# A fused window attention and two dense layers on one core: the reciprocal sums move to the PSUM banks of P^T, and the first loads are issued from two queues

## Chip, cores and metric

The kernel runs on one core of a Trainium2 chip. The metric is the device time of one execution in microseconds (us). TensorE is called PE here, VectorE DVE, ScalarE ACT, GpSimd POOL, and SyncE SP, as in the profile; PEld is PE's weight load, which has rows of its own.

## What is computed

Windowed causal attention (4 batches, 8 heads, 576 positions, head size 64, a window of 128 keys and a linear position bias), then two dense layers of 512 to 2048 to 512 on the 2304 rows that result. The first layer's activation is a quotient of polynomials, the second's a squared ReLU.

```python
scores = scale * q @ k.T                      # per head
scores = where(0 <= rel < 128, scores - slope * abs(rel), -1e9)
attn = exp(scores - max); attn /= attn.sum() + 1e-9
x = (attn @ v)                                # 2304 x 512
h = x @ w_in;   g = (a0 + a1 h + a2 h^2 + a3 h^3) / (1 + |b0||h| + |b1| h^2 + 1e-6);  y = g @ w_out
h = y @ w2_in;  g = max(h, 0)^2;  out = g @ w2_out
```

The weights come as 64-bit floats, so the kernel rebuilds each 32-bit value from two words.

## The kernel before

**Attention** works on 16 pairs of heads. For a pair, q and k are loaded as 128x4x128 blocks. PE transposes four q blocks into one PSUM bank (`tr_main`, line 337; called trq below), ACT or DVE copies the bank to `qkT` (`tr_copy`), the same follows for k (trk), and for the last 64 queries and keys together (`tr_rem`, trr). Three groups of score matmuls (`s_pe`) write four banks, five query tiles in all. DVE adds the bias and takes the row bound (`ttr`, line 383, tile `e`). ACT takes the exponential and its row sum (`exp`, into `sums`). PE transposes the probabilities (`pt_pe`, P^T, called ptp), and ACT or DVE copies them (`pt_copy`, called ptc, tile `ptsb`). PE multiplies by v (`pv_pe`) into bank `o`. The last 64 queries go into a bank `or`, which also holds the transposed reciprocal sums. `rcp` adds 1e-9 to the nine sums of a pair and takes the reciprocal, both on DVE. `r_tr` (plan name rtp) transposes them on PE into `or`. `r_copy` copies them out as `rt`, and `x_copy` copies `o` (plan name xo) and the last queries (xr) into `xT`. The result is stored unnormalised beside the reciprocals.

**PSUM** has eight banks here, handed out by `bank` (line 243): tag `s` has four, `pt` two (P^T), `o` one, `tr` one. trq, trk, trr and `or` take turns in the one bank `tr`.

**Weights** are rebuilt in 64 chunks beside all this: four steps on DVE, ACT or POOL (lines 206 to 218, tile `wb`) and a split into a rounded high part and a rest (lines 222 to 229). Eleven bits of precision in each part make three matmuls out of one.

**The dense layers** run in blocks of 512 rows (one of 256) and 16 steps per block: `gemm_in` (line 685) fills one of the four `s` banks (tile `h`) with 12 matmuls, some nine elementwise instructions on ACT, POOL and DVE follow, which end with `gl` on DVE, and `gemm_out` accumulates `y` in the banks of `pt`, `o` and `tr`. Step f of `gemm_in` needs the bank of step f-4, and so its `gl`. The first four steps need the score banks of the last pair.

**What sets the order** is the class `Plan` (lines 16 to 97). Every operation has its predecessors, a cost for each engine that may run it, and a priority. `run` takes again and again the operation that could start first by these costs; as `WEIGHT` is 0, the priority, with a number from the table `BIAS` added for each kind of operation, only decides between equal starts. The order found is written out, and each engine then works through its own list in order.

Of the kernel before, what the change touches and what calls it, by code (L numbers as in the profile page):

```python
# [8 lines left out]
F32 = mybir.dt.float32  # L9
# [3 lines left out]
ALU = mybir.AluOpType  # L13


class Plan:
# [30 lines left out]
    def run(self):  # L47
# [9 lines left out]
        while ready:  # L57
            best = None
            for name in ready:
                _, after, prio, engs, _, port = self.ops[name]  # L60
# [21 lines left out]
            if eng == "Pool" or (eng == "DVE" and self.ops[name][5]):  # L82
                free["port"] = max(free.get("port", 0.0), end - self.PORT[eng])
            if eng == "SP":
                free["DMA"] = max(free.get("DMA", 0.0), end + self.QUEUE) + self.ops[name][4]
                end = free["DMA"] + self.DONE
# [12 lines left out]

BIAS = {'W0': -416.9, 'W1': -833.9, 'W2': 174.9, 'W3': -153.9, 'attn_end': 896.0, 'bias': -332.0, 'exp': 84.0, 'g1': 159.6, 'g2': 163.5, 'gh': 2.9, 'gl': -268.1, 'ldk': 57.5, 'ldk0': -338.4, 'ldq': 99.3, 'ldq0': 331.9, 'ldr': 377.8, 'ldv': 105.8, 'ptc': -247.7, 'ptp': 268.5, 'pv': 64.8, 'r_abs': 33.0, 'r_g1': 63.2, 'r_g2': -144.0, 'r_g3': -694.3, 'r_p1': 486.9, 'r_p2': 266.4, 'r_r1': 109.8, 'r_r2': 206.0, 'r_t1': -202.8, 'r_t2': -379.6, 'r_u': -91.6, 'rcp': -171.9, 'rout': 202.1, 'rtc': -511.3, 'rtp': -541.3, 's': -127.0, 's_g': -91.3, 's_relu': -222.2, 'scl': -214.7, 'scp': 712.6, 'trk': 99.1, 'trk0': 101.2, 'trk0c': -324.6, 'trkc': 290.0, 'trq': -28.9, 'trq0': -378.1, 'trq0c': -90.4, 'trqc': 356.2, 'trr': 192.3, 'trrc': -666.1, 'ttr': -675.7, 'w0': 396.4, 'w1': 108.0, 'w2': 400.3, 'w3': -491.9, 'w4': -326.2, 'w5': -103.3, 'warm': 442.5, 'wl': -405.2, 'x': 124.7, 'xh': -413.4, 'xl': -200.5, 'xld': -1.2, 'xn': -207.3, 'xo': 145.8, 'xr': 36.3, 'yc': -225.0, 'yo': -531.9}  # L100
WEIGHT = 0.0000
# [7 lines left out]
def tile_window_attention_moe_moe(  # L109
# [20 lines left out]
    nc = tc.nc  # L130
# [169 lines left out]

    def load_qk(p, nme, src, t0, t1):
        b, hp = pairs[p]
        h0 = 2 * hp
        if t0 == 0:
            st[p][nme] = araw.tile([P, NQ - 1, 2, D], F32, tag=f"{nme}r", name=f"{nme}r{p}")
        t = st[p][nme]
        for j in range(2):
            nc.sync.dma_start(
                t[:, t0:t1, j, :], src[b, h0 + j, t0 * P : t1 * P, :].rearrange("(t p) d -> p t d", p=P)
            )  # L310

# [190 lines left out]
    for p in range(NP):  # L502
# [54 lines left out]
        for i in range(NQ):  # L557
# [3 lines left out]
            for j in range(2) if i < NQ - 1 else (1,):  # L561
# [6 lines left out]
                    ("exp", u, j), lambda u=u, j=j: exp(u, j), ACT=(0.49, 0.44, 0.39)[part],  # L568
                    after=[("ttr", u, j), ("rcp", p - 3)], prio=u,
# [21 lines left out]
        plan.add(("rtp", p), lambda p=p: r_tr(p), PE=0.08, after=[("rcp", p), ("trkc", p + 2), ("trrc", p + 1), ("xr", p - 1)], prio=u0 + 4.2)  # L591
        plan.add(
# [352 lines left out]
```

## Time and profile before

| | us |
|---|---|
| three runs | 943.40, 943.42, 945.23 |
| median | 943.42 |
| profiled execution | 942.65 |
| its span in the trace | 940.9 |
| PE busy | 923.6 (98%) |
| DVE busy | 625.9 (67%) |
| ACT busy | 494.9 (53%) |
| POOL busy | 324.0 (34%) |

The page also cuts the span into 40 slices with the busy share of each engine, lists the costliest groups of instructions, and follows the chain of work that ended last. Of that chain 87% lies on PE: 42% are the matmuls of line 778 (`y`) and 40% those of line 694 (`h`). A matmul's busy time overlaps with the next one's, so a PE that is busy all the time isn't at its peak by that alone; what counts is from one start to the next. The first 146 us are attention, the rest are the dense layers.

### The profile page before, as it was taken

To read this page: it belongs to the slowest core of one execution; us is meant where nothing else is said; L and a number is where in the kernel's file an instruction comes from. 1 tells how busy PE (TensorE), PEld (TensorE's weight loads), DVE (VectorE), ACT (ScalarE), POOL (GpSimd) and SP (SyncE) were. 2 spreads that over 40 slices of the span, in tenths; PEclk is the share of its full clock that TensorE was granted. 3 is DMA by queue.
4 is the path that set the end of the run, shared out by engine and by line. 5 is a ranking of instruction groups with operands and counts; after the bars stand their busy time and mean duration, and the time that the engine had idled before them with its cause. 6 is when DMAs were issued, how large, how long until landed. Compare 5 with 4: busy or idle time off the path is not lost.

```text
span 940.9 us, 14096 instructions
## 1 busy us (share of the span) xinstructions
PE 923.6 (98%) x4908; PEld 759.5 (81%) x4908; DVE 625.9 (67%) x1285; ACT 494.9 (53%) x1072; POOL 324.0 (34%) x343
## 2 busy tenths in 40 slices
PE   7999999999999999999999999999999999999998
PEld 5666667888998888888888888888888888888897
DVE  3999998999888886887799987862233223222232
ACT  4988887767767555655666654432222222222222
POOL 5354236867455446444666731030010001000000
PEclk9999999999999999999999999999999999999999
DMA  8999963322402100400142254302000200100010
GB/s 183 236 227 242 241 190 120 115 91 67 132 27 78 35 1 1 125 10 1 37 143 90 68 179 160 133 23 89 1 1 16 74 0 1 68 1 1 1 45 22
DMA packets 102311, 77.01 MB, mean 82 GB/s; under 512 B 64465, under 2 KB 89441, under 8 KB 102241
## 3 DMA queue, kind: packets, MB, share of 16 engines
q1 hardware_dynamic: 102240, 76.12, 28.7%
q8 instruction: 38, 0.62, 0.3%
q14 instruction: 33, 0.26, 0.1%
HBM read 61.87 MB, written 14.23 MB: 81 GB/s over the span
## 4 chain that ended last, share of the span: by engine, by line
PE 87%; DVE 8%; ACT 3%; DMA 1%; issue 1%; SPq 0%; POOL 0%; POOLq 0%; DVEq 0%; ACTq 0%
PE y L778 42%; PE h L694 40%; DVE e L391 3%; ACT e L407 2%; PE tr L340 1%; PE pt L442 1%; DVE wb L218 1%; PE warm L613 1%; DVE qkT L291 1%; DVE wb L216 1%; DMA win1r<-in_moe_w_in_dram 1%; DMA wout1r<-in_moe_w_out_dram 1%; PE o L468 0%; DVE ptsb L291 0%; DVE win1r L214 0%
## 5 line engine op out<-in xcount | busy, mean ns | idle before, releaser
L222 ACT ACTIVATE gh<-h 128x512 fp32r<-128x512 f32 (+1 forms) x160 | 88.7, 555 | 182.4 <-PE y L778 153.4
L229 DVE TENSOR_TENSOR gl<-h,gh 128x512 fp32r<-128x512 f32 (+1 forms) x160 | 101.7, 636 | 122.3 <-ACT gh L222 121.7
L755 DVE SCALAR_TENSOR_TENSOR h<-h,ah 128x512 f32<-128x512 f32 (+1 forms) x80 | 51.6, 645 | 115.0 <-ACT ah L751 114.8
L694 PE MATMUL h<-xh,win1hi 128*128 128x512 f32 (+1 forms) x320 | 118.1, 369 | 1.0 <-DVE gl L229 1.0
L694 PE MATMUL h<-xl,win1hi 128*128 128x512 f32 (+1 forms) x320 | 117.8, 368 | 0.0
L778 PE MATMUL y<-gh,wout1hi 128*128 128x512 f32 (+1 forms) x320 | 117.8, 368 | 0.0
L778 PE MATMUL y<-gl,wout1hi 128*128 128x512 f32 (+1 forms) x320 | 117.7, 368 | 0.0
L694 PE MATMUL h<-xh,win1lo 128*128 128x512 f32 (+1 forms) x320 | 117.7, 368 | 0.0
L778 PE MATMUL y<-gh,wout1lo 128*128 128x512 f32 (+1 forms) x320 | 117.7, 368 | 0.0
L694 PE MATMUL h<-xh,win2lo 128*128 128x512 f32 (+1 forms) x320 | 117.7, 368 | 0.0
L694 PE MATMUL h<-xl,win2hi 128*128 128x512 f32 (+1 forms) x320 | 117.7, 368 | 0.0
L694 PE MATMUL h<-xh,win2hi 128*128 128x512 f32 (+1 forms) x320 | 117.6, 368 | 0.0
L778 PE MATMUL y<-wout2hi,gh 128*128 128x512 f32 x288 | 112.2, 390 | 0.0
L778 PE MATMUL y<-wout2hi,gl 128*128 128x512 f32 x288 | 112.2, 390 | 0.0
L778 PE MATMUL y<-wout2lo,gh 128*128 128x512 f32 x288 | 112.1, 389 | 0.0
L751 ACT ACTIVATE ah<-h 128x512 f32<-128x512 f32 (+1 forms) x80 | 44.4, 554 | 120.9 <-PE h L694 120.4
L719 POOL TENSOR_SCALAR t<-ah,ab_sb 128x512 f32<-128x512 f32 (+1 forms) x80 | 61.7, 772 | 130.6 <-ACT ah L707 114.4
L721 POOL TENSOR_TENSOR t<-t,ah 128x512 f32<-128x512 f32 (+1 forms) x80 | 99.3, 1241 | 5.5
L226 POOL TENSOR_SCALAR xh<-xr 128x512 fp32r<-128x512 f32 (+1 forms) x20 | 13.2, 664 | 249.9 <-PE h L694 248.7
L407 ACT ACTIVATE e<-e,st 128x256 f32<-128x256 f32 (+1 forms) x144 | 67.0, 467 | 8.9 <-DVE st L391 8.7
L694 PEld LDWEIGHTS h<-xh,win1hi 128*128 128x128 f32 x320 | 60.4, 189 | 11.3 <-DVE gl L229 1.3
L694 PEld LDWEIGHTS h<-xh,win2hi 128*128 128x128 f32 x320 | 60.3, 189 | 10.6
(121 smaller groups left out, 1878.7 us busy)
## 6 DMA issues: line engine op xcount, KB each, us to landing
win1r<-in_moe_w_in_dram SPq DMA_DIRECT2D x16, 512.0 KB, 4.8
wout1r<-in_moe_w_out_dram SPq DMA_DIRECT2D x16, 512.0 KB, 3.5
win2r<-in_moe_w_in_dram SPq DMA_DIRECT2D x16, 512.0 KB, 3.8
wout2r<-in_moe_w_out_dram SPq DMA_DIRECT2D x16, 512.0 KB, 3.5
xs<-xT SPq DMA_DIRECT2D x16, 288.0 KB, 4.7
out_dram<-yt SPq DMA_DIRECT2D x18, 256.0 KB, 2.3
vr<-in_v_dram SPq DMA_DIRECT2D x32, 128.0 KB, 3.8
ys<-yt SPq DMA_DIRECT2D x16, 256.0 KB, 2.3
```

Source lines behind the costliest of these rows:

```text
L216: nc.vector.scalar_tensor_tensor(wb, wb, 3, lw, ALU.logical_shift_left, ALU.bitwise_or)
L222: nc.scalar.activation(dst, src, AF.Copy)
L226: nc.gpsimd.tensor_scalar(dst, src, 1.0, 1.0, ALU.mult, ALU.mult)
L229: (nc.vector if eng == "DVE" else nc.gpsimd).tensor_tensor(dst, a, b, ALU.subtract)
L391: nc.vector.tensor_tensor_reduce(d["e"][:, j, :w], d["s"] if last else d["s"][j], biasl[hp // 2][:, hp % 2, :w] if last else bias8[hp][:, ...
L407: nc.scalar.activation(e, e, AF.Exp, scale=-1.0, bias=s[:, j : j + 1], accum_out=sums[p % 3][:, c : c + 1],)
L694: nc.tensor.matmul(h[:, :n], a[:, c * P : (c + 1) * P], bb[:, :n], start=(m == 0), stop=(m == 3 * NCC - 1),)
L719: nc.gpsimd.tensor_scalar(gt("t", 2, ji, f), ah, ab_sb[:, 1:2], ab_sb[:, 0:1], ALU.mult, ALU.add)
L721: nc.gpsimd.tensor_tensor(tl["t", ji, f], tl["t", ji, f], ah, ALU.mult)
L751: nc.scalar.activation(gt("ah", 2, ji, f), tl["h", ji, f], AF.Relu)
L755: nc.vector.scalar_tensor_tensor(h, h, 0.0, tl["ah", ji, f], ALU.max, ALU.mult)
L778: nc.tensor.matmul(dst, a, bb, start=(f == 0 and m == 0), stop=(f == NF - 1 and m == 2))
```

## The change

Five things change.

- `or` comes from tag `pt` in place of `tr`. Its places in the order of P^T tiles are written out (`turns`): in each pair between the fourth ptp and the fifth, the sums of the pair before. A user of `pt` waits until the one two places back has been copied out (`two_back`). The waits of trq, trk and trr on the copies of `or` are gone.
- The addition of 1e-9 becomes an operation of its own on POOL (`plus`); DVE keeps the reciprocal. `exp` of three pairs later waits for `plus`, no longer for `rcp`.
- The q, k and v loads of the first two pairs, and the first batch's remainder, may be issued by SP or by ACT, whichever the planner takes.
- The planner counts a load's transfer also where ACT issues it.
- The table `BIAS` has other numbers for all kinds of operations.

No matmul, transpose or copy is added or taken away; of elementwise instructions 16 additions go from DVE to POOL. With the order, many instructions change their engine and place.

```diff
             if eng == "Pool" or (eng == "DVE" and self.ops[name][5]):
                 free["port"] = max(free.get("port", 0.0), end - self.PORT[eng])
-            if eng == "SP":
+            if self.ops[name][4]:
...
-BIAS = {
+BIAS = {
...
+    def queue(eng):
+        return nc.scalar if eng == "ACT" else nc.sync
+
-    def load_qk(p, nme, src, t0, t1):
+    def load_qk(eng, p, nme, src, t0, t1):
...
-            nc.sync.dma_start(
+            queue(eng).dma_start(
...
+    def plus(p):
+        t = st[p]["rc"] = ap2.tile([P, NSUM], F32, tag="rc", name=f"rc{p}")
+        nc.gpsimd.tensor_scalar(t, sums[p % 3], 1e-9, 1.0, ALU.add, ALU.mult)
+
     def rcp(p):
-        t = st[p]["rc"] = ap2.tile([P, NSUM], F32, tag="rc", name=f"rc{p}")
-        nc.vector.tensor_scalar(t, sums[p % 3], 1e-9, None, ALU.add)
-        nc.vector.reciprocal(t, t)
+        nc.vector.reciprocal(st[p]["rc"], st[p]["rc"])
...
     def r_tr(p):
-        st[p]["or"] = bank("tr", f"or{p}")
+        st[p]["or"] = bank("pt", f"or{p}")
...
+    def two(p, cost=1.15):
+        return {"SP": cost, "ACT": cost} if p < 2 else {"SP": cost}
+
+    turns = []
+    for p in range(NP):
+        turns += [("ptp", p * NQ + i) for i in range(NQ - 1)] + [("rtp", p - 1)] * (p > 0) + [("ptp", p * NQ + NQ - 1)]
+    turns.append(("rtp", NP - 1))
+    frees = [("ptc" if n == "ptp" else "xr", k) for n, k in turns]
+    two_back = {t: frees[max(0, m - 2) : max(0, m - 1)] + turns[max(0, m - 1) : m] for m, t in enumerate(turns)}
...
-                    PE=0.45 * w, after=[(f"ld{nme}{part}", p), last, ("xr", p - 3)], prio=u0 - 5 + n,
+                    PE=0.45 * w, after=[(f"ld{nme}{part}", p), last], prio=u0 - 5 + n,
...
-        plan.add(("trr", p), lambda p=p: tr_rem(p), PE=0.12, after=[last, ("xr", p - 2), ("ldr", b)], prio=u0 - 3)
+        plan.add(("trr", p), lambda p=p: tr_rem(p), PE=0.12, after=[last, ("ldr", b)], prio=u0 - 3)
...
-                after=[("exp", u, 0), ("exp", u, 1), ("ptc", u - 2), ("ptp", u - 1)], prio=u,
+                after=[("exp", u, 0), ("exp", u, 1)] + two_back["ptp", u], prio=u,
...
-            ("rcp", p), lambda p=p: rcp(p), DVE=0.16,
-            after=[("exp", u, j) for u in range(u0, u0 + NQ) for j in range(2)] + [("rtp", p - 2)], prio=u0 + 4.2, port=True,
+            ("plus", p), lambda p=p: plus(p), Pool=0.12,
+            after=[("exp", u, j) for u in range(u0, u0 + NQ) for j in range(2)] + [("rtp", p - 2)], prio=u0 + 4.2,
+        )
+        plan.add(("rcp", p), lambda p=p: rcp(p), DVE=0.2, after=[("plus", p)], prio=u0 + 4.2)
+        plan.add(("rtp", p), lambda p=p: r_tr(p), PE=0.08, after=[("rcp", p)] + two_back["rtp", p], prio=u0 + 4.2)
```

The order shows it at two places. The first is PE in the middle of attention, before: a pair's part from its multiplication by v to the next scores. `tr_6_0` with `qr` is trq of pair 6, with `kr` trk; `o` and `or` belong to pair 5.

```order
L468 MATMUL o_951<-ptsb_848,vr_694 64x256 x6
L349 MATMUL trr_974<-ident,rem_331 128x128
L442 MATMUL pt_976<-ident,e_938 128x128 x2
L442 MATMUL pt_981<-ident,e_941 128x128 x4
L340 MATMUL tr_6_0_994<-ident,qr_783 128x128 x4
L369 MATMUL s_2_1006<-qkT_857 64x192 x2
L442 MATMUL pt_1011<-ident,e_955 128x128 x4
L340 MATMUL tr_6_0_1021<-ident,kr_758 128x128 x4
L442 MATMUL pt_1032<-ident,e_961 128x128 x4
L437 MATMUL pt_1040<-ident,e_1018 128x128 x2
L420 MATMUL or_1044<-ident,rc_897 9x128
L468 MATMUL o_951<-ptsb_848,vr_694 64x128 x2
```

And after, from the transposes of q of pair 5 on:

```order
L447 MATMUL pt_774<-ident,e_712 128x128 x4
L343 MATMUL tr_5_0_786<-ident,qr_665 128x128 x4
L447 MATMUL pt_799<-ident,e_721 128x128 x4
L425 MATMUL or_807<-ident,rc_621 9x128
L473 MATMUL o_656<-ptsb_569,vr_246 64x128 x2
L482 MATMUL or_807<-ptsb_569,vr_246 64x64 x2
L486 MATMUL or_807<-ptsb_569,remv_150 64x64 x2
L343 MATMUL tr_5_0_822<-ident,kr_652 128x128 x4
L442 MATMUL pt_835<-ident,e_739 128x128 x2
L473 MATMUL o_842<-ptsb_754,vr_555 64x256 x6
L352 MATMUL trr_864<-ident,rem_316 128x128
L447 MATMUL pt_866<-ident,e_752 128x128 x2
```

Four users of bank `tr` in a pair became three, and there is more other work between one of them and the next. `s_2`, which needs the copy of trr, no longer follows it closely.

The second place is DVE at the start of the first dense layer. `u0_1` is tile u of block 0, step 1; `h0_0` to `gl0_0` are the last elementwise steps of step 0. Before, the rows up to `gl` of step 0:

```order
L218 SCALAR_TENSOR_TENSOR wb20_2430<-wout1r_4_2363,wb20_2430 128x512
L727 TENSOR_TENSOR u0_1_2454<-u0_1_2454,h0_1_2411 128x512
L747 SCALAR_TENSOR_TENSOR t0_0_2428<-t0_0_2428,h0_0_2388 128x512
L729 SCALAR_TENSOR_TENSOR u0_1_2454<-u0_1_2454,ca_sb_112,h0_1_2411 128x512
L747 SCALAR_TENSOR_TENSOR h0_0_2388<-t0_0_2428,h0_0_2388 128x512
L747 SCALAR_TENSOR_TENSOR h0_0_2388<-u0_0_2426,ca_sb_112,h0_0_2388 128x512
L727 TENSOR_TENSOR u0_2_2485<-u0_2_2485,h0_2_2435 128x512
L747 SCALAR_TENSOR_TENSOR t0_1_2452<-t0_1_2452,h0_1_2411 128x512
L229 TENSOR_TENSOR gl0_0_2512<-h0_0_2388,gh0_0_2494 128x512
```

And after:

```order
L218 SCALAR_TENSOR_TENSOR wb21_2432<-wout1r_5_2363,wb21_2432 128x512
L764 SCALAR_TENSOR_TENSOR h0_0_2382<-t0_0_2430,h0_0_2382 128x512
L746 SCALAR_TENSOR_TENSOR u0_1_2455<-u0_1_2455,ca_sb_112,h0_1_2406 128x512
L764 SCALAR_TENSOR_TENSOR h0_0_2382<-u0_0_2428,ca_sb_112,h0_0_2382 128x512
L744 TENSOR_TENSOR u0_2_2480<-u0_2_2480,h0_2_2436 128x512
L764 SCALAR_TENSOR_TENSOR t0_1_2453<-t0_1_2453,h0_1_2406 128x512
L746 SCALAR_TENSOR_TENSOR u0_2_2480<-u0_2_2480,ca_sb_112,h0_2_2436 128x512
L291 COPY ptsb15_2344<-pt79_2507 128x2x128
L764 SCALAR_TENSOR_TENSOR h0_1_2406<-t0_1_2453,h0_1_2406 128x512
L744 TENSOR_TENSOR u0_3_2504<-u0_3_2504,h0_3_2461 128x512
L764 SCALAR_TENSOR_TENSOR h0_1_2406<-u0_1_2455,ca_sb_112,h0_1_2406 128x512
L229 TENSOR_TENSOR gl0_0_2537<-h0_0_2382,gh0_0_2518 128x512
```

`gl` of step 0 stands behind five more instructions: work of steps 1 to 3, and the copy of the last P^T tile, which PE now makes after the first four steps of `gemm_in` and not ahead of them.

## Rows read from the trace of the kernel before

**Rows 1.** Stretches: busy time (and instructions) of each engine, PE's granted clock, DMA.

```profile
core 0: us, PE busy (x) PEld busy (x) DVE busy (x) ACT busy (x) POOL busy (x), PEclk, DMA share, GB/s
60.00:80.00 20.00, 18.98 (x175) 13.54 (x177) 18.98 (x65) 16.30 (x57) 10.68 (x11) 1.00 0.91 223
120.00:140.00 20.00, 19.43 (x180) 13.71 (x180) 18.22 (x73) 17.12 (x61) 7.72 (x9) 1.00 0.63 178
160.00:180.00 20.00, 20.00 (x90) 16.54 (x89) 20.00 (x33) 14.63 (x27) 16.26 (x15) 1.00 0.45 133
```

**Rows 2.** PE's waits, 10 to 146 us: us, times, longest; four of seven.

```profile
PE tr L340 <- DVE qkT L291: 2.3, 8, 0.6
PE s L369 <- DVE qkT L291: 1.6, 3, 1.0
PE s L380 <- DVE qkT L291: 0.9, 1, 0.9
...
PE or L420 <- DVE qkT L291: 0.4, 2, 0.2
```

**Rows 3.** The same waits as the weight loads (PEld) see them, the first and the last of seven.

```profile
PEld tr L340 <- DVE qkT L291: 5.4, 12, 0.8
...
PEld s L369 <- ACT qkT L289: 0.7, 1, 0.7
```

**Rows 4.** Order of time, start and duration in us: turns in bank `tr`, and PE's kinds.

```profile
118.56 0.42 PEld L442 LDWEIGHTS pt<-ident,e 128*128 128x128 f32 x4 [0.17 <-ACT ptsb L289]
...
122.14 1.06 PEld L468 LDWEIGHTS o<-ptsb,vr 128*64 128x64 f32 x12 [0.33 <-DVE st L391]
...
123.59 0.14 PEld L349 LDWEIGHTS trr<-ident,rem 128*128 128x128 f32 x1 [0.39 <-DVE st L391]
...
132.97 0.66 PE L340 MATMUL tr<-ident,qr 128*128 128x128 f32 x4
...
134.15 0.69 DVE L291 COPY qkT<-tr 128x512 f32<-128x512 f32 x1
...
135.10 0.60 PE L340 MATMUL tr<-ident,kr 128*128 128x128 f32 x4
```

**Rows 5.** Instructions by line, 10 to 146 us, DVE, then ACT: busy us, mean ns.

```profile
L291 DVE COPY qkT<-tr 128x512 f32<-128x512 f32 x18 | 12.4, 687 | 1.8 <-PE tr L340 1.0
L414 DVE TENSOR_SCALAR rc<-sums 128x9 f32<-128x9 f32 x16 | 5.4, 336 | 0.9 <-ACT e L407 0.9
...
L289 ACT ACTIVATE qkT<-tr 128x512 f32<-128x512 f32 x12 | 7.1, 591 | 1.2 <-PE tr L340 1.2
```

**Rows 6.** Order of time at the start: SP's issue of q, and PE.

```profile
2.78 1.02 SPq L308 DMA_DIRECT2D qr<-in_q_dram  x2
...
7.44 0.38 PE L340 MATMUL tr<-ident,qr 128*128 128x128 f32 x2
7.66 0.83 PE L613 MATMUL warm<-ident 128*128 128x128 f32 x6
```

**Rows 7.** DMA issues, 0 to 20 us: KB each, median us to landing.

```profile
qr<-in_q_dram SPq DMA_DIRECT2D x4, 64.0 KB, 2.5
```

**Rows 8.** Order of time at the start of the first dense layer.

```profile
146.04 0.48 PE L694 MATMUL h<-xh,win1hi 128*128 128x512 f32 x1
...
150.36 0.69 DVE L727 TENSOR_TENSOR u<-u,h 128x512 f32<-128x512 f32 x1 [1.86 <-ACT u L711]
...
157.11 0.65 PE L468 MATMUL o<-ptsb,vr 128*64 128x256 f32 x4
...
158.42 0.69 DVE L229 TENSOR_TENSOR gl<-h,gh 128x512 fp32r<-128x512 f32 x1
...
159.16 0.50 PE L694 MATMUL h<-xh,win1hi 128*128 128x512 f32 x1 [0.59 <-DVE gl L229]
```

**Rows 9.** Order of time: what POOL's port and queue do to a small DVE instruction.

```profile
144.32 1.69 POOL L229 TENSOR_TENSOR wout1lo<-wb,wout1hi 128x512 fp32r<-128x512 f32 x1
...
145.21 0.83 DVE L414 TENSOR_SCALAR rc<-sums 128x9 f32<-128x9 f32 x1 [0.33 <-ACT e L407]
```

More of the change, by code (lines that the diff above doesn't have):

```diff
@@ L97, in run @@
             fn(eng) if len(engs) > 1 else fn()
-BIAS = {'W0': -416.9, 'W1': -833.9, 'W2': 174.9, 'W3': -153.9, 'attn_end': 896.0, 'bias': -332.0, 'exp': 84.0, 'g1': 159.6, 'g2': 163.5, 'gh': 2.9, 'gl': -268.1, 'ldk': 57.5, 'ldk0': -338.4, 'ldq': 99.3, 'ldq0': 331.9, 'ldr': 377.8, 'ldv': 105.8, 'ptc': -247.7, 'ptp': 268.5, 'pv': 64.8, 'r_abs': 33.0, 'r_g1': 63.2, 'r_g2': -144.0, 'r_g3': -694.3, 'r_p1': 486.9, 'r_p2': 266.4, 'r_r1': 109.8, 'r_r2': 206.0, 'r_t1': -202.8, 'r_t2': -379.6, 'r_u': -91.6, 'rcp': -171.9, 'rout': 202.1, 'rtc': -511.3, 'rtp': -541.3, 's': -127.0, 's_g': -91.3, 's_relu': -222.2, 'scl': -214.7, 'scp': 712.6, 'trk': 99.1, 'trk0': 101.2, 'trk0c': -324.6, 'trkc': 290.0, 'trq': -28.9, 'trq0': -378.1, 'trq0c': -90.4, 'trqc': 356.2, 'trr': 192.3, 'trrc': -666.1, 'ttr': -675.7, 'w0': 396.4, 'w1': 108.0, 'w2': 400.3, 'w3': -491.9, 'w4': -326.2, 'w5': -103.3, 'warm': 442.5, 'wl': -405.2, 'x': 124.7, 'xh': -413.4, 'xl': -200.5, 'xld': -1.2, 'xn': -207.3, 'xo': 145.8, 'xr': 36.3, 'yc': -225.0, 'yo': -531.9}
+BIAS = {'W0': -182.3, 'W1': -7.0, 'W2': -339.5, 'W3': -63.2, 'attn_end': -492.9, 'bias': -223.8, 'exp': 965.6, 'g1': 150.1, 'g2': 156.6, 'gh': 192.7, 'gl': -91.4, 'ldk': -73.0, 'ldk0': 191.3, 'ldq': 8.4, 'ldq0': 449.8, 'ldr': 142.4, 'ldv': 394.0, 'plus': -113.6, 'ptc': -302.4, 'ptp': 88.6, 'pv': 371.6, 'r_abs': 479.6, 'r_g1': 334.2, 'r_g2': -80.4, 'r_g3': -184.9, 'r_p1': -26.7, 'r_p2': 149.2, 'r_r1': 455.5, 'r_r2': -175.0, 'r_t1': -226.9, 'r_t2': -167.3, 'r_u': 358.8, 'rcp': 199.2, 'rout': -170.0, 'rtc': 127.4, 'rtp': 158.5, 's': -200.2, 's_g': -278.3, 's_relu': -452.5, 'scl': -756.7, 'scp': -64.2, 'trk': 360.2, 'trk0': -69.8, 'trk0c': 304.8, 'trkc': 94.0, 'trq': 601.9, 'trq0': -329.1, 'trq0c': -137.6, 'trqc': -31.9, 'trr': -124.8, 'trrc': 116.9, 'ttr': -371.2, 'w0': 372.0, 'w1': 267.5, 'w2': -266.5, 'w3': -194.2, 'w4': 504.6, 'w5': -247.9, 'warm': 355.9, 'wl': -658.4, 'x': 387.2, 'xh': -312.6, 'xl': 217.5, 'xld': 163.2, 'xn': 430.1, 'xo': -618.3, 'xr': 186.4, 'yc': 426.3, 'yo': -821.3}
 WEIGHT = 0.0000
@@ L307, in load_qk, with load_rem @@
         for j in range(2):
-            nc.sync.dma_start(
+            queue(eng).dma_start(
                 t[:, t0:t1, j, :], src[b, h0 + j, t0 * P : t1 * P, :].rearrange("(t p) d -> p t d", p=P)
             )
-    def load_rem(b, srcs=(q, k, v)):
+    def load_rem(eng, b, srcs=(q, k, v)):
         rem[b] = araw.tile([P, H, D], F32, tag="rem", name=f"rem_{b}"), remv[b % 2]
         for dst, src in zip((rem[b][0][:LAST], rem[b][0][P - LAST :], rem[b][1][P - LAST :]), srcs):
-            nc.sync.dma_start(dst, src[b, :, MAIN:, :].rearrange("h p d -> p h d"))
+            queue(eng).dma_start(dst, src[b, :, MAIN:, :].rearrange("h p d -> p h d"))
     rem = {}
@@ L321, in tile_window_attention_moe_moe, with load_v @@
         nc.gpsimd.memset(t[: P - LAST], 0.0)
-    def load_v(p):
+    def load_v(eng, p):
         b, hp = pairs[p]
@@ L327, in load_v @@
         for j in range(2):
-            nc.sync.dma_start(
+            queue(eng).dma_start(
                 t[:, :, j, :], v[b, h0 + j, :MAIN, :].rearrange("(t p) d -> p t d", p=P)
@@ L512, in tile_window_attention_moe_moe @@
                     (f"ld{nme}{part}", p),
-                    lambda p=p, nme=nme, src=src, t0=t0, t1=t1: load_qk(p, nme, src, t0, t1),
-                    SP=1.15, move=1.46 * w,
+                    lambda eng="SP", p=p, nme=nme, src=src, t0=t0, t1=t1: load_qk(eng, p, nme, src, t0, t1),
+                    **two(p), move=1.46 * w,
                     after=[("trkc", p - 2), ("ld" + nme, p - 1)] + ([] if part else [("ldk0", p)]),
@@ L518, in tile_window_attention_moe_moe @@
         plan.add(
-            ("ldv", p), lambda p=p: load_v(p), SP=1.15, move=1.46,
+            ("ldv", p), lambda eng="SP", p=p: load_v(eng, p), **two(p), move=1.46,
             after=[("pv", u0 - VB * NQ + NQ - 1), ("ldv", p - 1)], prio=u0 - 6,
@@ L523, in tile_window_attention_moe_moe @@
             plan.add(
-                ("ldr", b), lambda b=b: load_rem(b), SP=1.9, move=2.2,
+                ("ldr", b), lambda eng="SP", b=b: load_rem(eng, b), **two(p, 1.9), move=2.2,
                 after=[("pv", u0 - NPAIR * NQ - 1), ("trr", p - NPAIR - 1), ("ldr", b - 1)] + [("ldk", 0)][:p == 0],
@@ L568, in tile_window_attention_moe_moe @@
                     ("exp", u, j), lambda u=u, j=j: exp(u, j), ACT=(0.49, 0.44, 0.39)[part],
-                    after=[("ttr", u, j), ("rcp", p - 3)], prio=u,
+                    after=[("ttr", u, j), ("plus", p - 3)], prio=u,
                 )
@@ L586, in tile_window_attention_moe_moe @@
         plan.add(
-            ("rcp", p), lambda p=p: rcp(p), DVE=0.16,
-            after=[("exp", u, j) for u in range(u0, u0 + NQ) for j in range(2)] + [("rtp", p - 2)], prio=u0 + 4.2, port=True,
-        )
-        plan.add(("rtp", p), lambda p=p: r_tr(p), PE=0.08, after=[("rcp", p), ("trkc", p + 2), ("trrc", p + 1), ("xr", p - 1)], prio=u0 + 4.2)
+            ("plus", p), lambda p=p: plus(p), Pool=0.12,
+            after=[("exp", u, j) for u in range(u0, u0 + NQ) for j in range(2)] + [("rtp", p - 2)], prio=u0 + 4.2,
+        )
+        plan.add(("rcp", p), lambda p=p: rcp(p), DVE=0.2, after=[("plus", p)], prio=u0 + 4.2)
+        plan.add(("rtp", p), lambda p=p: r_tr(p), PE=0.08, after=[("rcp", p)] + two_back["rtp", p], prio=u0 + 4.2)
         plan.add(
```

## The prediction, made blind

> **What bounds the kernel now.** I read the busy time by stretches first. From 160 us on PE works through 90 matmuls in 20.00 us without a gap, 0.222 us each, and the matmuls of the dense layers are the same before and after, so nothing is to be won there [rows 1]. DVE is busy 20.00 of 20.00 us in the same stretch, so the first dense layer has a second engine at its limit. Attention, the first 146 us, is the only place with slack: PE is busy 18.98 of 20 us, DVE 18.98, ACT 16.30 from 60 to 80 us. PE and DVE are nearly level there, and ACT is not far off.
>
> Then I read what PE waits for in attention. Seven rows name a copy of q^T, k^T or the remainder as the last releaser; they begin with 2.3 us and sum to 6.9 us [rows 2]. These are the turns in the one bank `tr`, or score matmuls behind such a copy. The weight loads see the same seven waits from 5.4 us down to 0.7, in sum 15.2 us, but count the ordinary pitch of PE with them [rows 3]. One such turn in order of time: trq at 132.97, its copy on DVE at 134.15 for 0.69, trk at 135.10 [rows 4]. The copy came late and PE had run out of other work.
>
> **The change part by part.** The sum is made against the profiled execution, 942.65 us, 0.77 under the median of 943.42.
>
> *Bank `tr`.* The four users in a pair become three, and the order puts more between them: trq and trk had one P^T tile and the last scores between them, now in most pairs the whole of `or` and its six matmul rows. I take the 6.9 us of PE's own rows as gone [rows 2], since PE's count starts only when nothing is left in the array. The bounds: 3 us if half of these waits only change their releaser, 15.2 us by the weight loads [rows 3].
>
> *Banks `pt`.* `or` holds one of two banks from the sums' transpose to the copy xr. In the order 2 us or more of other PE work stands between the last matmul into `or` and the next user of that bank. The copies in that time are `rt`, xo and xr; a full copy takes 0.69 on DVE [rows 4], so the wait is covered. Cost 0, if rt, xo and xr aren't queued behind more than one other instruction.
>
> *PE's order.* PE's list up to the first dense layer has 199 changes of kind of work for 192, and those from one transpose to another, which cost least, fall from 50 to 34. So 23 dearer turns are added. The idle before a weight load is 0.17 between transposes, 0.33 from scores to `o`, 0.39 from `o` to trr [rows 4]: a dearer turn costs 0.16 to 0.22 us more. Some kinds show no idle at all, so a turn costs 0 to 0.22, and I take 0.12: 2.8 us lost, between 0 and 5.
>
> *Addition to POOL.* DVE loses 16 instructions of 0.336, 5.4 us [rows 5], off PE's path. What comes instead is a wait of the reciprocal for POOL, with DVE's row maxima queued behind it. Such a case was there before: the addition took 0.83 in place of some 0.17 while POOL ran 1.69 us [rows 9]. Sixteen times the 0.66 would be 10.6 us of DVE, half of which POOL's idle half [rows 1] would spare; but the order leaves several DVE rows between the last exponential and the reciprocal. I take 0, with 2 us as the bad end.
>
> *Copies that change engine.* Up to the last row maximum DVE has ten fewer full copies of q^T and k^T (0.687 each, 6.9 us) and ACT ten more (0.591, 5.9 us) [rows 5]. ACT's share goes from 82% to some 87%, DVE's down. No gain by itself: PE is the engine that ends last here. The cover is ACT's remaining idle time.
>
> *First loads.* The first q is issued at 2.78 and takes two pieces until 3.80, 2.5 us to landing, so it is there at 6.3 [rows 6, 7]. PE transposes it at 7.44, directly behind the warm-up matmuls, six rows in 0.83 us. The warm-up ends it, not the load. The changed order has one warm-up (two rows, 0.28) fewer ahead of that transpose and one more two places later. I take 0.1 us won, between 0 and 0.3. ACT's ten issues stand where ACT is idle.
>
> The Trainium skill (Trainium Kernel Development and Optimization, Key Constraints) says that DMAs from SP, ACT and POOL run on the same 16 DMA engines, and that issuing from several saves only issue time. By that rule the second queue could save the issue time of the v load ahead of q, about 1.0 us, and the sum would be 0.9 lower. The warm-up row speaks against even that.
>
> *Start of the first dense layer.* Before, the first `h` starts at 146.04, u of its step 0 at 150.36 on DVE (4.3 later), `gl` of step 0 ends at 159.11, and only then may step 4 start, at 159.16, after 0.59 us of waiting for just this [rows 8]. So PE had 13.1 us from step 0 to step 4, 12.55 without the wait. After, more attention is left over behind step 3: eight more matmuls into `o` as the trace counts them (four took 0.65 [rows 8], so 0.9 to 1.3) and a P^T tile; PE's work is 13.9. These 1.35 us are no longer done ahead of the first `h`, so they count nothing themselves. DVE has five more instructions ahead of that `gl`, 3.1 us at the 0.63 to 0.69 of rows 8 with one half copy, so `gl` ends 4.3 + 8.75 + 3.1 = 16.1 after the first `h`. PE then waits 2.2 instead of 0.55: 1.65 us lost, between 0.5 and 4.
>
> **The sum.** -6.9 + 2.8 - 0.1 + 1.65 = -2.55. From 942.65 that is 940.1 for an execution like the profiled one, 940.9 for the median.
>
> **Rivals.** *DVE was the bound of attention.* DVE is as busy as PE [rows 1], and by the order sheds 15 additions (5.0), ten full copies (6.9) and 14 smaller ones against six additions to its list, about 12 us net up to the last maximum. If DVE sets the pace, the stage falls by that, and 943.42 - 12 + 1.65 is 933. Against it: PE's work from start to start leaves only some 10% of gaps, less than 12 us once 2.8 is added to it. The Trainium skill (Perfetto Trace Analysis, Identifying the Most-Contended Engine) would have PE judged by its weight loads, 13.54 of 20 us here, and the engine with the highest occupancy improved first, which is DVE; by that rule this rival is the likely one.
>
> *The gain is eaten at the handover.* DVE is at 20.00 of 20 from 160 us on [rows 1]. If attention ends earlier but DVE has its list of weight splits and polynomial steps still to do, steps 4 to 8 wait one after the other. With 4.5 us lost there in place of 1.65, and 2 of the 6.9 turned into waits for exponentials, the result is 943.42 - 2.55 + 2.85 + 2 = 945.7 at worst and about 943 in the middle: no change.
>
> *Slower: bank `o` comes back too late.* There is one. Work on PE between the last P^T matmul of a pair into it and the first of the next falls from about 2.3 us to about 1.4 in eight of fourteen pairs, by the order. In that time the copy xo has to wait its turn on ACT or DVE and take 0.6 to 0.69. The point is 0.5 us of queue: ahead of xo now stand `rt`, half a P^T copy and an exponential in places, up to 1 us. With 0.5 us in 14 pairs, 7 us, the time is 947.9; with half, 944.4. Against it: the same copy was covered before.
>
> **Chances.** Forecast 0.41 (mostly below 941.5, a little above), DVE as the bound, or all 15.2 us gone (932.6), 0.12, eaten at the handover 0.28, `o` or another queue that makes it slower 0.19. A measurement of this kernel can tell about 0.2%, 1.9 us, from no change. Faster by more: 0.34 of the forecast's 0.41 and the 0.12, together 0.46. Within: 0.07 and 0.28, 0.35. Slower: 0.19. The range leaves out the end of the first rival and of the last. Down from 940.9 it goes by half of the 8.3 us between the two counts of waits and 0.8 of cheaper turns, to 936; up by the two bad ends of turns and handover, 2.2 and 2.35, to 945.5.
>
> **What would show it.** In the changed profile: the seven rows of PE waits on copies of q^T and k^T sum to 2 us or less; the first `h` starts near 140.5 in place of 146.04; step 4 starts some 16 us later, with a wait of about 2 us for `gl`; the stretch from 160 us on still has 90 matmuls in 20 us. First transpose at 7.2. Wrong would be: PE's waits on `o` or on exponentials where those for `tr` were, a DVE that waits for `plus` on POOL, or an attention that ends at 146 again.

## The result and the profile after

The changed kernel takes 947.67 us (median of 6 runs, 946.59 to 952.24), the kernel before 943.41 in the same session (942.34 to 945.23): a ratio of 1.0053, 95% interval 1.0032 to 1.0074. It is slower by half a per cent. The forecast was 940.9, faster, with a range up to 945.5; sign and range were both wrong.

The profiled execution of the changed kernel is its slowest, 952.24 us (span 950.3). Three kernels below have its order of attention, but for one store or the last P^T, and start the first `h` at 144.7 to 145.8; this execution starts it at 150.24. The 4.5 us between are its own, about what it lies above the median. Places in the order are read from it below, sums from the times.

The stretches of the changed kernel, columns as in [rows 1]; the first has no counterpart there:

```profile
10.00:20.00 10.00, 6.81 (x39) 4.10 (x41) 5.83 (x23) 4.98 (x19) 0.90 (x2) 0.83 1.15 201
60.00:80.00 20.00, 17.88 (x160) 12.42 (x162) 14.44 (x52) 15.50 (x51) 8.27 (x11) 1.00 0.93 213
...
160.00:180.00 20.00, 17.62 (x87) 13.44 (x86) 18.77 (x33) 14.11 (x27) 12.09 (x13) 0.91 0.25 81
```

Where [rows 1] has 90 matmuls in 20.00 us from 160 on, there are 87 in 17.62, and the granted clock (the column behind POOL) is 0.91; from 10 to 20 us it is 0.83. Two cuts, chosen where the clock fell, show its lower level:

```profile
16.20:19.40 3.20, 3.20 (x14) 1.70 (x14) 2.58 (x5) 2.42 (x10) 0.00 (x0) 0.50 1.00 181
166.50:169.60 3.10, 3.02 (x7) 2.44 (x8) 3.10 (x8) 1.45 (x3) 0.48 (x1) 0.50 0.25 95
```

0.50 is 1.2 GHz. The kernel before has 1.00 in every stretch up to the end.

PE's waits from 10 to 151 us, the answer to [rows 2] (us, times, longest); six of ten:

```profile
PE pt L447 <- ACT e L410: 4.0, 5, 2.6
PE s L372 <- ACT win1hi L222: 1.2, 1, 1.2
...
PE o L473 <- DVE xT L291: 1.0, 1, 1.0
PE or L425 <- ACT ptsb L289: 0.7, 2, 0.5
PE o L473 <- ACT xT L289: 0.7, 1, 0.7
PE tr L343 <- DVE qkT L291: 0.5, 1, 0.5
```

The waits on copies of q^T and k^T, 6.9 us before, are down to 0.5. That part went as forecast, and so did the copies that change engine, the answer to [rows 5] (here from 8 to 151 us):

```profile
L289 ACT ACTIVATE qkT<-tr 128x512 f32<-128x512 f32 x22 | 12.9, 587 | 1.2 <-PE tr L343 1.2
...
L291 DVE COPY qkT<-tr 128x512 f32<-128x512 f32 x8 | 5.5, 685 | 0.6 <-PE tr L343 0.4
```

New at the top of the waits is a P^T that waits for an exponential, 2.6 of its 4.0 us in one piece. It stands at the start, here in order of time (start, duration, engine, instruction, idle time before it and what ended it):

```profile
10.39 1.79 PE L383 MATMUL s<-qkT 64*128 64x128 f32 x16
10.61 2.20 ACTq L311 DMA_DIRECT2D kr<-in_k_dram  x2
13.26 0.93 ACTq L311 DMA_DIRECT2D qr<-in_q_dram  x2
14.24 0.40 ACT L410 ACTIVATE e<-e,st 128x128 f32<-128x128 f32 x1 [6.54 <-DVE st L394]
14.79 0.33 PE L447 MATMUL pt<-ident,e 128*128 128x128 f32 x1 [2.61 <-ACT e L410]
```

The same place in the kernel before:

```profile
11.90 0.40 ACT L407 ACTIVATE e<-e,st 128x128 f32<-128x128 f32 x1 [0.93 <-DVE st L391]
...
12.45 0.33 PE L442 MATMUL pt<-ident,e 128*128 128x128 f32 x1 [0.17 <-ACT e L407]
```

Between the scores and the first exponential ACT now issues the loads of pair 1's k and q. The chain of waits of the stretch 6 to 24 us (start, duration, what) tells what held these issues:

```profile
5.95 0.63 SPq L319
...
6.62 6.62 DMA remv<-in_v_dram
...
13.26 0.37 ACTq L311
...
13.68 0.52 ACTq L311
...
14.24 1.39 ACT e L410 x6
```

An issue on ACT stood until a transfer that SP had issued at 6.62 had landed at 13.24. Issuing takes 0.4 to 0.5 us each; waiting to issue held ACT's list from 7.7 to 14.2.

The program that the kernel is built into says why. Its 388 loads and stores, on SP and ACT alike, take eight semaphores in turn to signal that they have landed, and each issue first waits for the transfer that had its semaphore before, eight places earlier. For the first piece of pair 1's q on ACT this is `remv`, a load of SP. So it is the program that ties ACT to a load of SP here.

The start of the first dense layer, the answer to [rows 8]:

```profile
150.24 0.50 PE L711 MATMUL h<-xh,win1hi 128*128 128x512 f32 x1
...
155.37 0.67 DVE L744 TENSOR_TENSOR u<-u,h 128x512 f32<-128x512 f32 x1
...
161.16 0.74 DVE L764 SCALAR_TENSOR_TENSOR h<-u,ca_sb,h 128x512 f32<-128x512 f32 x1
...
162.84 0.44 PE L442 MATMUL pt<-ident,e 128*128 128x128 f32 x2
163.85 0.57 ACT L222 ACTIVATE gh<-h 128x512 fp32r<-128x512 f32 x1
...
165.85 0.68 DVE L229 TENSOR_TENSOR gl<-h,gh 128x512 fp32r<-128x512 f32 x1
...
166.58 0.79 PE L711 MATMUL h<-xh,win1hi 128*128 128x512 f32 x1 [1.91 <-DVE gl L229]
167.18 0.63 PE L711 MATMUL h<-xl,win1hi 128*128 128x512 f32 x1
```

Step 4 starts 16.3 us after step 0 (before: 13.1) after a wait of 1.91 us, and its matmuls then come every 0.43 us where they come every 0.23 at 2.4 GHz. Seven of them, from 166.58 to 169.69, cost 1.5 us more.

So there were two suspects of some 4 us and 3 us: ACT's loads at the start, and the handover from attention to the dense layer, each a stand of PE with a half clock behind it. A third was a store: at 78.61 ACT had stood 2.26 us ahead of a copy of x.

### The profile page after: what moved, and what is told of

Read it like the earlier page. It is cut to its first block, busy times and chain, and to the rows that moved or that the text cites. A ratio compares the mean times of both kernels' runs of the same rounds, so it can differ in the third digit from the quotient of the medians.

```text
span 950.3 us, 14033 instructions
## 1 busy us (share of the span) xinstructions
PE 930.3 (98%) x4908; PEld 761.5 (80%) x4908; DVE 619.4 (65%) x1261; ACT 496.5 (52%) x1082; POOL 323.3 (34%) x357
## 4 chain that ended last, share of the span: by engine, by line
PE 79%; DVE 10%; DMA 4%; ACT 3%; issue 2%; POOL 1%; SPq 1%; ACTq 0%; DVEq 0%; POOLq 0%
PE y L795 37%; PE h L711 37%; DVE h L764 2%; PE o L473 2%; DMA win1r<-in_moe_w_in_dram 2%; PE pt L447 1%; DVE e L394 1%; DVE t L764 1%; PE s L383 1%; ACT e L410 1%; DVE wb L218 1%; DVE u L746 1%; DVE wb L216 1%; DVE gl L229 1%; DVE u L744 1%
## 5 line engine op out<-in xcount | busy, mean ns | idle before, releaser
L711 PEld LDWEIGHTS h<-xh,win1hi 128*128 128x128 f32 x320 | 60.7, 190 | 13.4 <-DVE gl L229 3.3
L711 PEld LDWEIGHTS h<-xl,win1hi 128*128 128x128 f32 x320 | 60.8, 190 | 10.2
```

Of the source, the lines that this page charges most:

```text
L711: nc.tensor.matmul(h[:, :n], a[:, c * P : (c + 1) * P], bb[:, :n], start=(m == 0), stop=(m == 3 * NCC - 1),)
```

## The experiments

All times are medians beside runs of the kernel before on the same chip; ratios are to that kernel. Its medians were 942.9 to 944.1.

**Pair 1's loads back on SP.**

```diff
             fn, _, _, engs, _, _ = self.ops[name]
+            if name in (("ldk", 1), ("ldq", 1)):
+                eng = "SP"
```

> The changed kernel with the four loads of pair 1's q and k issued by SP again, at the same places of the order; nothing else moves. Theory A (ACT's in-order queue is held by these loads): in the changed kernel ACT issues the last of them at 13.68, behind the landing of an earlier load, and begins its first exponential at 14.24, 2.3 us later than before (11.90), while PE waits 2.6 us and then runs for 3.4 us at half the clock (granted 0.5 from 16.1 to 19.5 us). With the loads on SP the first exponential starts at about 12.0, PE's wait there falls below 1 us, no half clock follows, and the time falls by 2.3 and 1 to 1.7 us, part of which is given back later: 943.5 to 946 after 947.7. Theory B (the start is hidden, the loss sits in PE's changed order and its turns): the first exponential comes earlier, but the first h still starts at 150 and the time stays at 947 to 948.5.

Measured: 944.00 us, ratio 1.0006 (0.9998 to 1.0015), 3.7 us less than the changed kernel (4.4 by the ratios); granted clock 1.00 over the profiled span. Its rows at the start, and the first `h`:

```profile
11.80 0.40 ACT L412 ACTIVATE e<-e,st 128x128 f32<-128x128 f32 x1 [3.90 <-DVE st L396]
12.35 0.33 PE L449 MATMUL pt<-ident,e 128*128 128x128 f32 x1 [0.17 <-ACT e L412]
...
141.40 0.50 PE L713 MATMUL h<-xh,win1hi 128*128 128x512 f32 x1
...
157.74 0.50 PE L713 MATMUL h<-xh,win1hi 128*128 128x512 f32 x1 [1.91 <-DVE gl L231]
```

Theory A holds. The first `h` is 4.6 us earlier than before, near the 140.5 of the forecast. The wait of 1.91 at step 4 is still there. No half clock follows it in this execution (1.00 from 140 to 200 us); of the eleven runs, four had a mean clock of 0.999 or 1.0 and took 941.93 to 943.18, seven had 0.997 or 0.998 and took 943.98 to 944.59.

**The split of a weight chunk behind `gl` of step 0; a store early; and all three.** The first two, in the changed kernel:

```diff
-            after=[("wl", n), was], prio=pr, port=True,
+            after=[("wl", n), was] + [("gl", 0, 0)] * (n >= 21), prio=pr, port=True,
```

```diff
+        order = [(58.85 if o[2] == ("x", 3) else o[0], *o[1:]) for o in order]
         for _, _, name, eng in sorted(order):
```

> The changed kernel with the split of weight chunk 21 (three DVE instructions, 2.3 us) ordered behind gl of step 0 in the first dense layer; what stands ahead of the first h is the same. Theory A (the handover costs what PE waits for gl of step 0, and the half clock behind that wait): in the changed kernel step 4 starts at 166.58 after 1.9 us of PE waiting, and its first seven matmuls take 0.43 us instead of 0.23 (granted clock 0.5 for 3.4 us). With gl 2 us earlier the wait is below 0.5 us, the seven matmuls run at 0.23, and the time falls by 1.5 to 3.6 us: 944 to 946. Theory B (DVE is the limit of the first dense layer anyway, so a wait removed here comes back at a later step): the wait at step 4 goes, another of about the same size comes between steps 5 and 20, time 947 to 948.5.

> The changed kernel with one store, pair 3's x to DRAM, issued by SP right behind that pair's reciprocal sums and thus ahead of eleven other issues; nothing else moves. In the changed kernel this store is issued 10 us after its data are there, and ACT stands 2.3 us (76.3 to 78.6) ahead of the copy of pair 5's x, which takes the same buffer; PE then waits 0.7 us for bank o. Theory A (ACT waits for that store): the 2.3 us on ACT are gone, PE's wait for bank o too, and attention ends 0.7 to 2 us earlier, time 945.7 to 947. Theory B (ACT waits there for something else): ACT still starts that copy at 78.6, time as the changed kernel, 947 to 948.5.

> The three edits together: pair 1's loads on SP, the split of chunk 21 behind gl of step 0, pair 3's store early. If the loss of the changed kernel sits in these three places, the gains add: 947.7 - 3 - 2.5 - 1.2 = 941, between 939 and 943, at or below the kernel before (943.4), with a granted clock of 1.0 over the span. If the places only hide one another (an engine behind them sets the end), the sum falls short and the time stays at 944 or more.

Measured: 956.12 (ratio 1.0138, 1.0125 to 1.0152), 948.26 (1.0051, 1.0034 to 1.0068), 947.20 (1.0058, 1.0037 to 1.0080). Neither edit gains, and the three together are slower than pair 1's loads on SP alone.

The first edit moves more than three instructions. The list `after` feeds the planner, which plans all that follows anew; some sixty places in DVE's list and forty in ACT's differ. The three instructions of the split are gone from ahead of `gl` of step 0, but two others came in their place, so that DVE has one less there, and step 4 started 16.9 us after step 0, after 2.3 us of waiting. The five instructions that the prediction blames (work of steps 1 to 3, and the copy of the last P^T) all still stand ahead of `gl`, so this run says nothing on them. The loss came later: from the first `h` (144.70) to the end of the span (953.4) this kernel takes 808.7 us, the changed kernel 800.1. PE's waits of that kernel from 200 to 310 us:

```profile
PE h L711 <- DVE gl L229: 6.2, 6, 1.8
PE y L795 <- DVE gl L229: 1.0, 1, 1.0
```

That these waits come from the splits that were put back is likely (theory B), but not shown. With the store early ACT's 2.26 us are gone and the time is the same; but kernels with the changed order whose store stays late waited 0 to 1.1 us there too. That wait is scatter of single executions, not the cause.

**The last P^T ahead of the first `h`.** Something else that can hold `gl` is in the order of PE. The exponentials live in the buffers of `gh` and `gl` (tag `("gh", "gl")[u % 2]`), so `gh` of step 0 waits for the transposes that read the last ones. Before, these stood ahead of the first `h`; after, behind step 3 (162.84 above, `gh` 163.85).

```diff
-                after += [("s", NP - 1, 2), ("exp", NU - 1, 1)] + [("ttr", NU - 1 - u, 1) for u in range(NQ)]
+                after += [("s", NP - 1, 2), ("exp", NU - 1, 1)] + [("ttr", NU - 1 - u, 1) for u in range(NQ)] + [("ptp", NU - 1)]
```

> The changed kernel with the last P^T tile's transposes put back ahead of the first h of the first dense layer, as the kernel before has them; in the changed kernel they missed that place, because their PSUM bank comes free only with the copy of the tile before them, and stand behind step 3. The buffers of gh are those of the exponentials, so gh of step 0 can't be written before these transposes have read them. Theory A (this place costs the handover): step 4 starts some 13.3 us after the first h instead of 16.3, PE's 1.9 us wait for gl of step 0 and the half clock behind it (1.7 us) are gone; the copy ahead may cost 0.3 us of waiting before the first h; time 947.7 less 3.3, 943.5 to 945.5. Theory B (DVE's own list sets gl of step 0): step 4 still starts 16 us after the first h, time 947 to 948.5.

> The changed kernel with both edits: pair 1's loads on SP (alone 944.0) and the last P^T tile ahead of the first h. If the rest of the loss is the handover, step 4 starts at about 141.5 + 13.3 = 155 (before: 159.2), the granted clock is 1.0 over the whole span, and the time is 944.0 less 2 to 3.3: 940.7 to 942, under the kernel before by 0.1 to 0.25%. This is what was predicted for the change itself (the waits on bank tr gone, first h near 140.5). If DVE is the bound from the first h on, the gain is given back by step 20 and the time is 943.5 to 944.5.

Measured: 945.59 (ratio 1.0020, 1.0009 to 1.0032) and, with pair 1's loads on SP as well, 940.95 (0.9972, 0.9962 to 0.9983). Rows of the second:

```profile
141.72 0.41 PE L444 MATMUL pt<-ident,e 128*128 128x128 f32 x2
141.89 0.48 PE L713 MATMUL h<-xh,win1hi 128*128 128x512 f32 x1
...
153.78 0.59 ACT L224 ACTIVATE gh<-h 128x512 fp32r<-128x512 f32 x1
...
154.54 0.68 DVE L231 TENSOR_TENSOR gl<-h,gh 128x512 fp32r<-128x512 f32 x1
...
155.28 0.50 PE L713 MATMUL h<-xh,win1hi 128*128 128x512 f32 x1
```

`gl` ends 13.3 us after the first `h` instead of 16.3, step 4 starts at 13.4 without a wait, and no half clock follows. Theory A holds for the place, but the edit doesn't show by what the place acts. It is planned anew as well: with the transposes ahead, `gh` moves forward on ACT, and on DVE only two instructions are left between the last `h` of step 0 and `gl`, as in the kernel before, in place of seven. The rows of the changed kernel show both at work: the last `h` ended at 161.90, `gh` at 164.42, and DVE worked without a gap until it came to `gl` at 165.85. So `gh`, which the planner puts behind the transposes (they end at 163.28), held `gl` back up to 164.42, and DVE's list for the last 1.4 us.

Both edits together (the fast version, below) beat both kernels; a second session gave a little less:

> The changed kernel with pair 1's loads on SP and the last P^T tile ahead of the first h, beside the kernel before on the same chip as the two runs that follow: the ratio to the kernel before was 0.9972; if it holds from chip to chip, it is 0.996 to 0.9985 here, and the first h starts near 142.

Measured: 942.17 beside 943.10, ratio 0.9982 (0.9969 to 0.9994), first `h` at 143.5. The two sessions together say 0.998, some 2 us under the kernel before.

**One part alone in the kernel before.** Pair 1's loads on ACT, the bank of `or`, the addition on POOL, and the other first loads on ACT; each keeps every place in the order.

```diff
-            nc.sync.dma_start(
+            (nc.scalar if p == 1 else nc.sync).dma_start(
```

```diff
-        st[p]["or"] = bank("tr", f"or{p}")
+        st[p]["or"] = bank("pt", f"or{p}")
```

```diff
-        nc.vector.tensor_scalar(t, sums[p % 3], 1e-9, None, ALU.add)
+        nc.gpsimd.tensor_scalar(t, sums[p % 3], 1e-9, 1.0, ALU.add, ALU.mult)
```

```diff
-            nc.sync.dma_start(
+            (nc.scalar if p == 0 and nme == "q" and t0 else nc.sync).dma_start(
...
-            nc.sync.dma_start(
+            (nc.scalar if p < 2 else nc.sync).dma_start(
```

> The kernel before with one part of the change alone: the four loads of pair 1's q and k are issued by ACT, at the same places in the order. Theory A (ACT is held by these issues until earlier loads have landed, whatever the rest of the order): the first exponential moves from 11.9 to 14 or later, PE waits 2 us or more ahead of the first P^T and runs at half clock behind that, time 942.9 plus 2.3 to 3.7, 945 to 946.6. Theory B (only the changed order is hurt by it): the first exponential stays near 12, time 942.3 to 943.7.

> The kernel before with the bank alone changed: the transposed sums and the last queries' result go to the banks of P^T, and every instruction keeps its place in the order. If the bank itself is what PE waits for, the waits on q^T and k^T copies (6.9 us on PE) shrink and the time falls by 3 us or more, 940 or less. If the order is what matters (trk still stands close behind trq's copy, and the next P^T now stands behind the copy of the last queries' result), those waits stay above 4 us, others on P^T banks come, and the time is 942.5 to 945.

> The kernel before with the addition to the sums on POOL alone, at the same place in the order. If the addition on DVE is what costs (3 us in the changed kernel with both edits, when it was put back on DVE), the time falls by 1 to 3 us, a ratio of 0.997 to 0.999. If the gain there needs the changed order (several DVE instructions between the addition and the reciprocal, which here follow each other directly, so that DVE waits for POOL's 0.4 to 1.3 us instructions), the time stays or rises, 0.9995 to 1.004.

> The kernel before with v and the rest of q of pair 0 and v of pair 1 issued by ACT, which is idle then; pair 1's q and k stay on SP. In the changed kernel with both edits, putting these on SP cost 0.4%. If that gain comes from SP being done earlier with its own list, it shows here too: ratio 0.996 to 0.999. If it belongs to the changed order, which counts on the second queue, the ratio is 0.9995 to 1.0015.

Measured: 950.15 (ratio 1.0069, 1.0052 to 1.0086), 945.76 (1.0024, 1.0013 to 1.0035), 942.84 (0.9992, 0.9982 to 1.0001) and 943.00 (0.9994, 0.9984 to 1.0005).

The loads cost more than expected, 6.7 us. In the kernel before, ACT also copies the first q^T and k^T, and the last of these copies stood behind the issues. PE's first scores broke off in the middle, and the chain shows the same step as above, a landing that releases an issue on ACT:

```profile
9.90 0.93 PE L380 MATMUL s<-qkT 64*128 64x128 f32 x8
18.31 2.08 PE L380 MATMUL s<-qkT 64*128 64x256 f32 x8 [7.48 <-ACT qkT L289]
```

```profile
8.95 8.48 DMA remv<-in_v_dram
...
17.45 0.38 ACTq L308
...
17.87 0.39 ACT qkT L289
```

The bank alone makes the kernel slower, by a little more than expected. PE's waits up to 150 us there, four of thirteen:

```profile
PE tr L340 <- DVE qkT L291: 2.6, 8, 0.7
PE or L420 <- ACT ptsb L289: 1.8, 4, 0.5
PE s L369 <- DVE qkT L291: 1.6, 3, 1.0
...
PE pt L437 <- DVE xT L291: 1.0, 1, 1.0
```

trk still stands close behind trq's copy, and the waits on copies of q^T and k^T are still 6.4 us (6.9 before); `or` and the next P^T now wait for each other's copies. That the gain needs the changed order is likely, but the changed order with `or` left in bank `tr` was not run. The addition and the other loads change nothing that can be told from zero. For the addition DVE's waits say why, 10 to 150 us:

```profile
DVE rc L415 <- POOL rc L414: 5.2, 7, 1.5
```

DVE is rid of 5.4 us of additions [rows 5] and waits 5.2 us for POOL instead, because here the reciprocal follows at once.

**The half clock, and two parts taken back out of the fast version.**

```diff
     def pt_pe(u):
+        if u == 0:
+            for _ in range(16):
+                nc.tensor.matmul(tl["warm"][:, :P], ident, ident, start=True, stop=True)
```

```diff
-        nc.gpsimd.tensor_scalar(t, sums[p % 3], 1e-9, 1.0, ALU.add, ALU.mult)
...
+        nc.vector.tensor_scalar(st[p]["rc"], sums[p % 3], 1e-9, None, ALU.add)
         nc.vector.reciprocal(st[p]["rc"], st[p]["rc"])
```

```diff
+            if eng == "ACT" and str(name[0])[:2] == "ld":
+                eng = "SP"
```

> The changed kernel with the last P^T tile ahead of the first h (alone 945.6; pair 1's loads still on ACT), and 16 more warm-up matmuls on PE between the first scores and the first P^T, where PE otherwise stands 2.0 us until the first exponential. They add no work behind that wait. Theory A (PE's stand is what the half clock follows, granted 0.5 for 3.4 us from 17.6 on): the first exponential stays at 14 or later, the granted clock is 1.0 over the span, and the time falls by the 1 to 1.7 us of the half clock, 943.9 to 944.6. Theory B (the half clock has to do with the start of the kernel, not with this stand): the half clock stays, time 945 to 946.5.

> The changed kernel with pair 1's loads on SP and the last P^T tile ahead of the first h (940.95), and the addition to the sums back on DVE, right ahead of the reciprocal; all else in its place. If the addition costs PE nothing on either engine, as predicted, the time stays within 940 to 942. If DVE was a bound of attention, the 16 additions of 0.17 to 0.34 us come back as 2.7 to 5.4 us, 943.5 or more. If the wait of the reciprocal for POOL cost something, the time falls, 940 or less.

> The same kernel (940.95) with the remaining first loads of ACT (v and the rest of q of pair 0, v of pair 1) on SP as well, so that the second queue is gone. If the second queue brings nothing (the first transposes stand behind the warm-up matmuls, as predicted 0.1 us), the time stays within 940.3 to 941.8. If it brings the issue time of the v load ahead of the first q (two pieces, about 1 us), the time is 941.5 to 942.5.

Measured: 944.53 (ratio 1.0007, 0.9998 to 1.0016), 944.07 (1.0004, 0.9995 to 1.0013), 944.93 (1.0010, 1.0000 to 1.0020), in a session where the kernel before took 944.11, so the ratios are what to compare. PE at the start of the first:

```profile
9.98 1.79 PE L383 MATMUL s<-qkT 64*128 64x128 f32 x16
11.70 3.84 PE L439 MATMUL warm<-ident 128*128 128x128 f32 x32
15.38 0.85 PE L450 MATMUL pt<-ident,e 128*128 128x128 f32 x6
```

```profile
16.00:19.40 3.40, 3.21 (x21) 1.52 (x20) 3.14 (x6) 3.09 (x11) 0.09 (x1) 1.00 1.14 185
```

The exponential was as late as before (13.87), the filling even longer than the wait (32 rows as the trace counts them, 3.84 us), and still the time fell from a ratio of 1.0020 to 1.0007, 1.2 us, with a granted clock of 1.00. The intervals overlap, so the size is rough. That this half clock goes with the stand and not with the start is shown by the row, and by the mean clocks: 1.0 in nine of eleven executions and 0.998 in two, where all eleven of the same kernel without the filling had 0.996 to 0.998.

The addition back on DVE costs 0.22 to 0.32% against the two sessions of the fast version, 2.1 to 3 us: the first `h` comes at 143.1 and PE again waits 1.2 us for `gl` at step 4. All loads on SP cost 0.28 to 0.38%, 2.6 to 3.6 us. The first transpose is 0.15 us later, no more; SP is late with its own list, and PE waits 1.0 us for a later q. Behind this wait the clock is halved again, for some 3.4 us:

```profile
PE tr L345 <- DMA qr<-in_q_dram: 1.0, 1, 1.0
```

```profile
26.20:29.20 3.00, 3.00 (x15) 2.67 (x14) 2.02 (x5) 1.29 (x6) 0.85 (x2) 0.50 1.00 212
```

Eight of the eleven executions had a mean clock of 0.995 to 0.998; with the second queue it was two of eleven, both 0.998. So part of what the second queue gains is a half clock that doesn't come.

## Why the prediction was wrong, point by point

*Bank `tr`, -6.9.* Right in kind. PE's waits on these copies fell from 6.9 to 0.5; in the fast version all of PE's waits up to the first `h` are 5.0 us in place of 10.2.

*PE's dearer turns, +2.8.* Of those 5.2 us the first `h` shows 4.1 (141.89 for 146.04; in the second session, at 143.5, 2.6), and 0.9 to 1.3 of these are the `o` matmuls left for later. So -4.1 was put for what measured between -1.3 and -3.2. The same gain also holds what the addition and the other loads bring, so what the turns cost isn't shown.

*First loads, -0.1, with ACT's issues "where ACT is idle".* **This is the step that failed.** I looked at when ACT has nothing to compute, and not at what an issue waits for, nor at what is queued behind it on ACT: the first exponentials. The row that I costed at 0.1 us of gain held 3.6 to 4.5 us of loss in pair 1's four issues. The other loads gain 2.6 to 3.6 us with the changed order, through SP's later loads and the clock, and not through the first transpose (6.83 us without the second queue, 6.68 with it).

On this the Trainium skill (Trainium Kernel Development and Optimization, Key Constraints) says that issuing from several queues saves only the issue time. In size the other loads agree with it: six issues of some 0.5 us left SP, 3 us in all, and 2.6 to 3.6 were gained in the changed order, the clock included. Pair 1's four issues cost more than that, because ACT stood until the transfers that they wait for had landed.

*Start of the dense layer, +1.65.* The wait was as forecast: `gl` ended 16.3 us after the first `h` (forecast 16.1), the wait was 1.91 (2.2). The reason was in part luck. The five DVE instructions do hold `gl`, but only for the last 1.4 us; up to then it could not have come even without them, because `gh` stood behind the last P^T, the work that I had noted as counting nothing by itself. Left out altogether was the half clock that can follow the stand, 1.5 us by its rows. By the ratios this place, with the order planned anew behind it, costs 2.3 to 3.2 us. Even without it the layer isn't as fast as before: from the first `h` to the end of the span the kernel before takes 794.9 us, the changed kernel 800.1, and the one with both edits 797.3 and 796.7 in its two sessions, of which the `o` matmuls are 0.9 to 1.3.

*Addition, 0.* Nothing in the kernel before, but 2 to 3 us in the fast version. Why so much is open; 1.2 us of it are the wait for `gl`.

*Rivals.* DVE was not the bound of attention: from 60 to 80 us its 18.98 us fell to 14.44 in the changed kernel and to 16.43 in the one with both edits, and of the 12 us of this rival the first `h` there shows 2.6 to 4.1. Bank `o` came back late only in single executions (1.7 us in the profiled one), and is not what made the kernel slower. "Eaten at the handover" was the right place for less than half of it. The loss at the start had no rival.

The account: kernel before 943.4; what the change is about, less 2 (ratio 0.998); pair 1's loads on ACT, plus 3.6 to 4.5 (two pairs of kernels, by ratios); the last P^T behind step 3, plus 2.3 to 3.2. Sum 947.3 to 949.1, measured 947.7. These terms are differences between the same kernels, so the sum checks only that the two losses add up, whichever is taken out first; they do. What stays open: why the profiled execution lost some 4.5 us more in attention, 2.26 of which ACT waited ahead of the copy of x; and how much of the remaining 2 us of gain each part holds, since no part alone gives any in the kernel before.

## What to carry to other kernels

Before a load moves to the queue of an engine that computes, ask what its issue waits for (here the landing of the transfer eight places earlier, on whichever queue) and what is queued behind it, not whether the engine is idle there. A load whose issue has to wait belongs to a queue with nothing urgent behind it. Work that is deferred past a boundary is free only if no buffer of the next stage waits for it. A stand of PE of 1 to 2.6 us, as here, can be paid twice, once as the wait and once as the clock behind it. And an edit to what a planner reads can move much more than it names: compare the orders before reading the time.

## What the hardware showed that was not expected

- A load can take far longer to land than the first ones do: `remv`, issued by SP, took 6.62 us here and 8.48 in the kernel before with pair 1's loads on ACT, where the first q took 2.5 [rows 7]. With the program's eight semaphores an issue on ACT stood for it (13.24 to 13.26, and 17.43 to 17.45).
- PE's granted clock fell to 0.5 for 3.4 us near two stands of PE, 2.61 us up to 14.79 (it fell at 16.0) and 1.91 us up to 166.58 (it fell at 166.2). In the profiled executions it stayed at 1.00 with the first stand filled, and with both gone; with the second alone left it fell in some executions and not in others. With all loads on SP it fell at 26.1, behind two shorter stands, 1.2 us up to 23.21 and 1.0 up to 25.99.
